# Block attention with a soft mixture of experts: another order of the work inside an attention turn, another chain between the last turn and the experts, and second-matrix loads of 1 MB

## The chip, the cores and the metric

The kernel runs on one core of one Trainium2 chip. The metric is the device time of one execution in microseconds (us). A core has a matrix engine (PE, with its weight loads shown as PEld), a vector engine (DVE), a scalar engine (ACT), GpSimd (POOL) and SyncE (SP, which here issues every load and store). Each engine works through its own instructions in program order; engines wait for each other through semaphores. All numbers are float32.

## The reference, cut to what matters

```python
# q, k, v: (8, 8, 576, 64); attention inside chunks of 64 rows
scores = scale * np.matmul(q_c, k_c.transpose(0, 1, 2, 4, 3))
attn = softmax(scores); out = np.matmul(attn, v_c)
x = out.transpose(0, 2, 1, 3).reshape(4608, 512)
# soft mixture: 8 experts with 4 slots each, phi (512, 32)
logits = x @ phi
d = softmax over the 4608 rows of logits        # per slot
slot_input = d.T @ x                             # (32, 512)
slot_out[e] = np.maximum(slot_input[e] @ w1[e], 0) @ w2[e]   # w1 (8,512,1024), w2 (8,1024,512)
c = softmax over the 32 slots of logits          # per row
return c @ slot_out                              # (4608, 512)
```

## The kernel before, in words

The 4608 rows are cut into nine blocks of 512. Blocks 0 to 7 are the first 512 rows of one batch each; the ninth gathers the last 64 rows of all eight batches and is worked on fifth. A **turn** is two heads of one block, so there are 36 turns, four to a block, and turns 16 to 19 belong to the gathered block.

In a turn the two heads of q and k are brought side by side by POOL (`pair_heads`, tiles `kp`, `qp`), transposed by PE into the PSUM banks `pg` and `ph` (`turn_qk`) and copied by ACT to `kT` and `qT` (`place_qk`, line 217). PE makes the scores in `psc` (`scores`, 227, 32 matmuls), DVE subtracts the maximum (`s_sub`, 233 and 234), ACT takes the exponential (`s_exp`, 239), PE transposes the result into `pt` (`turn_p`, 245), ACT copies it to `at` (`place_p`, 248), PE multiplies by the values into `pav` (`values`, 259), DVE divides (`norm_x`, 272 to 274), PE transposes the row result into `px` (`turn_x`, 280) and ACT copies it to `xT` (`place_x`, 283). POOL lays the values out twice before they are used (`spread_v`, 185 to 190). The code of one pass of the loop works on several turns at once: scores of t, values of t-1, q and k of t+1 and t+2, row result of t-2. `sc`, `at`, `kT`, `qT`, `kp`, `qp` and the PSUM banks are single.

Once for each block, spread over four passes, the bank `pg` also serves the mixture: `logits` with the running maximum and the exponentials (`maxima`, `weights`), two transposes (`natural`), the block's share of the slot inputs (`partial`, added to `p_run`), and the combination weights (`combination` on POOL, then `turn_c`, `place_c` into `cT`).

The order of all instructions is written by hand; nothing reorders it. SP issues in code order: pieces of weights (512 KB each, paced by the pass number: 34 pieces before turn 33), `load_v` of turn t+2 for two turns at a time, `load_qk` of turn t+5. A load waits until its buffer has been read (values have two buffers of two turns, q and k three of one turn) and until the load eight before it has landed. The gathered block is loaded in smaller pieces: eight of 64 KB for two turns of values, four of 128 KB for a turn of q and k.

Behind the last turn a chain of small steps leads from the last row result to the slot inputs `siT`; the softmax over rows is finished there across four lanes (`lane_minimum`, `lane_weights`, `lane_select`), and `slots` makes `siT`. Then the experts: `up` for two experts at a time reads the first matrix (16 tiles of 1 MB, all in SBUF by then), `turn` transposes, `down` reads the second matrix. Of the 32 weight tiles 17 lie in pool `wpa` and are loaded during the turns. Six more go into `wpb`, which lies over the buffers of the attention part and is loaded as these come free. The last nine go into `wpa` again (`refill`), each when `up` has read the tile that lay there. Then the rows are combined and stored.

## Time and profile before

| | us |
|---|---|
| median of three runs | 262.9 (262.69 to 264.4) |
| profiled execution, its own time | 264.01 |
| its span, first to last instruction | 262.2 |
| PE busy in it | 211.6 (81%) |
| DVE, ACT, POOL busy | 123.6, 124.9, 122.2 |
| bytes moved | 71.97 MB, 274 GB/s over the span |

Busy shares are means over the whole span. The span has three parts: the turns, up to about 179 us; the chain and the experts, up to about 230 us; combination and stores. The share of the DMA engines in a stretch is the time that its packets took, over the time of 16 engines; packets overlap, so it can pass 1.

### The profile page before, as it was taken

The page shows a single profiled execution, that of the slowest core. Times are in us where ns is not written, and L with a number is a line of the kernel's source. Part 1 is how long each engine was busy: PE and PEld are TensorE (multiplying, and loading weights), DVE is VectorE, ACT ScalarE, POOL GpSimd, SP SyncE. Part 2 cuts the span into 40 slices and gives each one's busy share as a digit, 9 for nine tenths or more (in the row PEclk, how much of TensorE's full clock was granted, in tenths as well). Part 3 has the DMA queues.
Part 4 walks back from the last instruction along what each step waited for, and adds up shares of the span by engine and source line. Part 5 has one row for each costly group of instructions (what it writes and reads, how often), then busy time and mean ns, then how long its engine had stood idle before and what let it go on. Part 6 is the DMA issues. An engine that isn't in the chain of part 4 may idle for free.

```text
span 262.2 us, 9367 instructions
## 1 busy us (share of the span) xinstructions
PE 211.6 (81%) x3828; PEld 151.6 (58%) x3828; DVE 123.6 (47%) x303; ACT 124.9 (48%) x277; POOL 122.2 (47%) x315
## 2 busy tenths in 40 slices
PE   7788898998988837798897997986579999979700
PEld 7676776675865727577676776674242346447400
DVE  0265656676666631765855956675310000136800
ACT  1447665666666542667567666664111210135600
POOL 2686877865583718397577885850030000000000
PEclk9999999999999995999999999999757999986965
DMA  6978999998974959988999999356956999587997
GB/s 208 317 210 242 357 324 343 303 268 255 296 215 123 274 140 302 356 264 269 358 309 286 345 300 366 94 162 209 391 203 217 356 349 348 177 284 245 264 366 286
DMA packets 60090, 71.97 MB, mean 274 GB/s; under 512 B 3728, under 2 KB 50832, under 8 KB 60048
## 3 DMA queue, kind: packets, MB, share of 16 engines
q1 hardware_dynamic: 60048, 71.38, 85.5%
q8 instruction: 30, 0.49, 0.7%
q14 instruction: 12, 0.10, 0.1%
HBM read 61.93 MB, written 9.44 MB: 272 GB/s over the span
## 4 chain that ended last, share of the span: by engine, by line
PE 46%; DMA 12%; POOL 11%; ACT 11%; DVE 9%; issue 5%; SPq 1%; ACTq 0%; POOLq 0%; DVEq 0%
PE ph L538 6%; PE po L572 5%; PE pf L599 5%; PE pt L245 5%; PE pg L198 4%; PE pav L259 4%; DMA vna<-in_v_dram 4%; ACT sc L239 3%; PE psc L227 3%; PE pg L290 3%; DMA qn<-in_q_dram 3%; DMA knb<-in_k_dram 3%; PE ph L143 3%; ACT kT L217 2%; DMA vnb<-in_v_dram 2%
## 5 line engine op out<-in xcount | busy, mean ns | idle before, releaser
L217 ACT COPY kT<-pg 128x512 f32<-128x512 f32 x36 | 21.1, 587 | 43.9 <-PE pg L198 42.9
L233 DVE TENSOR_REDUCE mx<-psc 128x8 f32<-128x512 f32 x36 | 24.8, 690 | 36.1 <-PE psc L227 36.0
L248 ACT COPY at<-pt 128x512 f32<-128x512 f32 x36 | 21.1, 586 | 21.0 <-PE pt L245 21.0
L198 PE MATMUL pg<-ident,kp 128*128 128x128 f32 x144 | 23.5, 287 | 6.1 <-DVE eT L337 4.1
L245 PE MATMUL pt<-ident,sc 128*128 128x128 f32 x144 | 23.8, 289 | 5.2 <-ACT sc L239 3.8
L234 DVE TENSOR_TENSOR sc<-psc,mx 128x512 f32<-128x512 f32 x36 | 24.9, 692 | 3.2
L227 PE MATMUL psc<-kT,qT 64*64 64x64 f32 x1152 | 25.4, 224 | 0.8 <-ACT qT L217 0.7
L274 DVE TENSOR_TENSOR xb<-pav,rc 128x512 f32<-128x512 f32 x36 | 24.9, 691 | 1.2
L245 PEld LDWEIGHTS pt<-ident,sc 128*128 128x128 f32 x144 | 15.5, 142 | 17.1 <-ACT sc L239 9.7
L227 PEld LDWEIGHTS psc<-kT,qT 64*64 64x64 f32 x1152 | 20.3, 134 | 7.0 <-ACT qT L217 4.2
L239 ACT ACTIVATE sc<-sc 128x512 f32<-128x512 f32 x36 | 22.8, 633 | 0.6 <-DVE sc L234 0.6
L198 PE MATMUL ph<-ident,qp 128*128 128x128 f32 x144 | 22.4, 279 | 0.2 <-issue 0.2
L280 PE MATMUL px<-ident,xb 128*128 128x128 f32 x144 | 22.2, 278 | 0.0
L259 PE MATMUL pav<-vnb,at 64*64 64x65 f32 x576 | 13.7, 229 | 10.4 <-POOL vnb L190 5.7
L194 POOL COPY qp<-qn 128x512 f32<-128x512 f32 x36 | 22.0, 612 | 0.2 <-DMA qn<-in_q_dram 0.2
L198 PEld LDWEIGHTS pg<-ident,kp 128*128 128x128 f32 x144 | 15.4, 142 | 9.4 <-issue 3.8
L217 ACT COPY qT<-ph 128x512 f32<-128x512 f32 x36 | 20.7, 576 | 0.0
L259 PEld LDWEIGHTS pav<-vnb,at 64*64 64x64 f32 x576 | 11.3, 138 | 12.8 <-POOL vnb L190 6.0
L194 POOL COPY kp<-knb 128x512 f32<-128x512 f32 x24 | 14.7, 611 | 8.3 <-PE pg L198 6.4
L280 PEld LDWEIGHTS px<-ident,xb 128*128 128x128 f32 x144 | 17.1, 143 | 1.0 <-ACT xTa L283 0.8
L198 PEld LDWEIGHTS ph<-ident,qp 128*128 128x128 f32 x144 | 17.0, 143 | 1.0 <-POOL vna L188 0.4
L538 PE MATMUL ph<-w,siT 128*32 128x512 f32 x128 | 17.2, 692 | 0.0
(96 smaller groups left out, 344.9 us busy)
## 6 DMA issues: line engine op xcount, KB each, us to landing
w<-in_moe_w_dram SPq DMA_DIRECT2D x64, 512.0 KB
qn<-in_q_dram SPq DMA_DIRECT2D x32, 256.0 KB
knb<-in_k_dram SPq DMA_DIRECT2D x21, 256.0 KB
vna<-in_v_dram SPq DMA_DIRECT2D x16, 256.0 KB
vnb<-in_v_dram SPq DMA_DIRECT2D x16, 256.0 KB
out_dram<-ob SPq DMA_DIRECT2D x8, 512.0 KB
out_dram<-ob SPq DMA_DIRECT2D x4, 1024.0 KB
kna<-in_k_dram SPq DMA_DIRECT2D x11, 256.0 KB
```

The costliest lines, as they stand in the source:

```text
L194: nc.gpsimd.tensor_copy(dst.rearrange("p j a d -> p a j d"), src)
L198: nc.tensor.transpose(out=dst[:, P * j:P * (j + 1)], in_=(kp if isk else qp)[:, j].rearrange("p a d -> p (a d)"), identity=ident)
L217: nc.scalar.copy(o, i)
L227: nc.tensor.matmul(psc[CH * m:CH * (m + 1), a, o:o + CH], lhsT=qT[r, c], rhs=kT[r, c], start=True, stop=True)
L233: nc.vector.reduce_max(mx, pv, axis=AX.X)
L234: nc.vector.tensor_tensor(sc.rearrange("p a M (w x) -> p a (M w) x", x=CH), pv, mx.unsqueeze(3).to_broadcast([P, 2, 4, CH]), ALU.subtract)
L239: nc.scalar.activation(sc, sc, AF.Exp, scale=SCALE)
L245: nc.tensor.transpose(out=pt[:, o:o + P], in_=sc[:, a, M], identity=ident)
L259: nc.tensor.matmul(pvv[q_, 2 * w + M, a, 0:D + 1], lhsT=at[r, a, M, q_], rhs=values_of(t)[r, M, a, 2 * D * m:2 * D * m + D + 1], start=Tru ...
L274: nc.vector.tensor_tensor(x_of(t).rearrange("p l (a d) -> p l a d", d=D), pvv[:, :, :, 0:D], rc.to_broadcast([P, 4, 2, D]), ALU.mult)
L280: nc.tensor.transpose(out=px[:, P * l:P * (l + 1)], in_=x_of(t)[:, l], identity=ident)
L538: nc.tensor.matmul(ph[SL * i:SL * (i + 1), :], lhsT=siT[:, j, :], rhs=wt[1, e, j // 2][:, j % 2, DM * h:DM * (h + 1)], start=(j == 0), sto ...
```

## The change: what it does

**A turn in another order.** In a pass, `turn_p` and `place_p` of turn t-1 now come directly behind the scores of t, and no longer those of turn t behind everything else. `values` of t-1 comes last on PE, directly in front of the next pass's scores. On POOL `pair_heads` of t+2 is now ahead of `spread_v` of t. On SP `load_qk` is now ahead of `load_v`. The mixture's steps are kept together, ahead of the values.

**Another chain behind the last turn.** The logits of the last block are begun before its last row result is there; the transpose of the previous combination weights gets a bank of its own; `lane_minimum` comes ahead of `weights`; the last `partial` is done and added in two halves; five small matmuls on `ident` (`warm`) are added; and the last block's combination weights are transposed behind the first `up` instead of ahead of it, copied by DVE and not by ACT.

**Loads.** The nine full tiles of the second matrix outside the first 17 are loaded by one transfer of 1 MB each, not two of 512 KB. Half tiles of the first matrix are ordered by use: both experts' first halves, then both second halves.

```diff
-    worder = [(1, e, h) for e in range(E) for h in range(2)]
+    worder = [(1, e0 + i, h) for e0 in range(0, E, 2) for h in range(2) for i in range(2)]
...
-            return [(t[:, 1024 * i:1024 * (i + 1)], src[:, 1024 * i:1024 * (i + 1)]) for i in range(2)]
+            return halves(t, src) if n < NWA else [(t, src)]
...
             if t < NT:
                 scores(t)
+            if t >= 1:
+                turn_p(t - 1)
+                place_p(t - 1)
+            if t < NT:
                 s_sub(t)
+            if t + 1 < NT:
+                turn_qk(t + 1, 1, pg)
+                place_qk(t + 1, 1, pg)
+                turn_qk(t + 1, 0, ph)
+                place_qk(t + 1, 0, ph)
+            if t + 2 < NT:
+                pair_heads(t + 2, 1)
+                pair_heads(t + 2, 0)
+            if t + 5 < NT:
+                load_qk(t + 5)
+            if t < NT:
+                s_exp(t)
                 spread_v(t)
+            if t >= 2:
+                turn_x(t - 2)
...
             if t >= 1:
                 values(t - 1)
                 norm_x(t - 1)
             if t % 2 == 0 and t + 2 < NT:
                 load_v(t + 2)
...
-            if t < NT:
-                turn_p(t)
-                place_p(t)
             if t >= 2:
                 place_x(t - 2)
...
+        n = NB - 1
+        logits(n, ph, range(NF - 1))
         turn_x(NT - 1)
         place_x(NT - 1)
-        n = NB - 1
-        turn_c(n - 1)
-        place_c(n - 1)
-        logits(n)
-        maxima(n)
-        weights(n)
+        turn_c(n - 1, psc[:, 0])
+        place_c(n - 1, psc[:, 0])
+        logits(n, ph, range(NF - 1, NF))
+        maxima(n, ph)
+        warm(2)
         wmin = lane_minimum()
+        weights(n, ph)
+        warm(2)
         natural(n)
         natural_copy(n)
         wj = lane_weights(*wmin)
         sums(n)
+        for h in range(2):
+            partial(n, pt, slice(DH * h, DH * (h + 1)))
         ss = lane_select(wj)
-        partial(n, pt)
-        partial_add(n, pt)
+        for h in range(2):
+            partial_add(n, pt, slice(DH * h, DH * (h + 1)))
+        warm(1)
+        slots(*ss)
         shifted(n)
-        slots(*ss)
         combination_exp(n)
         combination(n)
-        turn_c(n)
-        place_c(n)
...
-    load_pieces(wpb, 2 * NWB)
+    load_tiles(wpb, NWB)
...
         hrs[e] = up(e)
+        if e == 0:
+            pc = bank("pc")
+            nc.tensor.transpose(out=pc[:, 0:P], in_=eT, identity=ident)
+            nc.vector.tensor_copy(cT[:, order_b[NB - 1]], pc[:, 0:P])
```

On PE a pass with `partial`, from the scores of one turn to those behind the next, stood like this before (`psc` scores, `pav` values, `pg` and `ph` the transposes of k and q, `px` the row result, `pt` the exponentials):

```order
L227 MATMUL psc<-kT,qT 64x64 x16
L259 MATMUL pav<-vnb_94,at 64x65 x16
L198 MATMUL pg<-ident,kp 128x128 x4
L198 MATMUL ph<-ident,qp 128x128 x4
L280 MATMUL px<-ident,xb_103 128x128 x4
L360 MATMUL pg<-xb_92,eN 32x512 x4
L245 MATMUL pt<-ident,sc 128x128 x4
L227 MATMUL psc<-kT,qT 64x64 x16
```

The same pass on PE now:

```order
L239 MATMUL psc<-kT,qT 64x64 x16
L257 MATMUL pt<-ident,sc 128x128 x4
L210 MATMUL pg<-ident,kp 128x128 x4
L210 MATMUL ph<-ident,qp 128x128 x4
L292 MATMUL px<-ident,xb_104 128x128 x4
L372 MATMUL pg<-xb_93,eN 32x512 x4
L271 MATMUL pav<-vnb_95,at 64x65 x16
L239 MATMUL psc<-kT,qT 64x64 x16
```

The transposes of the exponentials moved from the pass's end to behind the scores and belong to the turn before; the values moved from behind the scores to the end.

On SP two passes stood like this before (late in the turns, behind the gathered block):

```order
L171 DMA vnb_94<-in_v_dram 128x4x128 x2
L154 DMA knb_99<-in_k_dram 128x2x256
L154 DMA qn_86<-in_q_dram 128x2x256
L103 DMA w_6_0_2102<-in_moe_w_dram 128x1024
L154 DMA kna_87<-in_k_dram 128x2x256
L154 DMA qn_84<-in_q_dram 128x2x256
L103 DMA w_6_1_2259<-in_moe_w_dram 128x1024
```

The same two passes on SP now:

```order
L166 DMA knb_100<-in_k_dram 128x2x256
L166 DMA qn_87<-in_q_dram 128x2x256
L183 DMA vnb_95<-in_v_dram 128x4x128 x2
L114 DMA w_6_0_2097<-in_moe_w_dram 128x1024
L166 DMA kna_88<-in_k_dram 128x2x256
L166 DMA qn_85<-in_q_dram 128x2x256
L114 DMA w_7_0_2254<-in_moe_w_dram 128x1024
```

The two loads of values moved behind one load of k and one of q.

On PE the end of the chain, from the transposed maximum to the first matmuls of `up`, was before:

```order
L374 MATMUL psc<-ident,nm_run_71 1x128
L327 MATMUL pg<-ident,eT 128x128
L328 MATMUL pg<-ident,lT 128x128
L389 MATMUL psc<-one,wj 128x32
L360 MATMUL pt<-xb_103,eN 32x512 x4
L400 MATMUL ph<-wsel,p_run 128x32 x4
L405 MATMUL px<-ws,rep 128x1
L353 MATMUL pg<-ident,eT 128x128
L538 MATMUL ph_3235<-w_0_0_280,siT 32x512 x2
```

And now:

```order
L386 MATMUL psc<-ident,nm_run_71 1x128
L155 MATMUL px<-ident 128x128 x2
L339 MATMUL pg<-ident,eT 128x128
L340 MATMUL pg<-ident,lT 128x128
L372 MATMUL pt<-xb_104,eN 32x256 x8
L401 MATMUL pav<-one,wj 128x32
L155 MATMUL px<-ident 128x128
L411 MATMUL ph<-wsel,p_run 128x32 x4
L416 MATMUL pav<-ws,rep 128x1
L548 MATMUL ph_3237<-w_0_0_275,siT 32x512 x2
```

The transpose of `eT` in front of `up` is gone from here, and the partial product now precedes the lanes' weights.

## Rows read from the trace of the kernel before

**Rows 1.** Windows by stretch: bounds and length (us), busy time (instructions) of PE, PEld, DVE, ACT, POOL; granted clock, DMA share, GB/s.

```profile
9.59:60.28 50.69, 43.94 (x997) 35.31 (x998) 30.23 (x68) 31.92 (x66) 39.91 (x104) 1.00 0.96 296
60.28:104.61 44.33, 34.87 (x728) 27.74 (x727) 23.90 (x58) 24.28 (x54) 25.87 (x65) 0.92 0.77 224
104.61:165.66 61.05, 53.32 (x1179) 41.10 (x1178) 40.34 (x98) 39.47 (x88) 42.96 (x108) 1.00 0.99 316
165.66:179.26 13.60, 11.60 (x301) 9.52 (x301) 8.19 (x20) 9.16 (x21) 7.64 (x21) 1.00 0.30 91
193.40:199.00 5.60, 5.28 (x25) 1.37 (x29) 0.00 (x0) 0.27 (x1) 2.29 (x9) 0.50 0.06 23
199.00:225.60 26.60, 26.34 (x332) 11.92 (x324) 1.16 (x8) 2.75 (x4) 0.00 (x0) 0.98 1.05 346
```

**Rows 2.** Timeline of PE: scores of turns 12, 20, 33, values of the last turn.

```profile
60.28 0.69 PE L227 MATMUL psc<-kT,qT 64*64 64x64 f32 x32
...
104.61 0.69 PE L227 MATMUL psc<-kT,qT 64*64 64x64 f32 x32
...
165.66 0.69 PE L227 MATMUL psc<-kT,qT 64*64 64x64 f32 x32
...
178.56 0.70 PE L259 MATMUL pav<-vnb,at 64*64 64x65 f32 x32 [0.78 <-issue]
```

**Rows 3.** The chain that ended last through one pass: start, length, what.

```profile
48.26 0.69 PE pav L259 x32
...
49.58 0.45 ACT kT L217
...
50.06 0.64 ACT sc L239
...
50.75 0.66 PE pt L245 x4
51.40 0.62 PE psc L227 x32
```

**Rows 4.** Timeline of POOL: first and last step of one pass.

```profile
65.86 0.40 POOL L185 COPY vna<-vna 128x256 f32<-128x256 f32 x1
...
68.84 0.61 POOL L194 COPY qp<-qn 128x512 f32<-128x512 f32 x1
```

**Rows 5.** Timelines of SP and POOL: a load of values and its first reader.

```profile
135.69 0.93 SPq L171 DMA_DIRECT2D vna<-in_v_dram  x2
...
144.07 0.40 POOL L185 COPY vna<-vna 128x256 f32<-128x256 f32 x1 [1.04 <-DMA vna<-in_v_dram]
```

**Rows 6.** Timelines of SP, POOL, PE: values of turn 18, load to use.

```profile
86.67 7.97 SPq L175 DMA_DIRECT2D vnb<-in_v_dram  x8
...
97.27 0.40 POOL L185 COPY vnb<-vnb 128x256 f32<-128x256 f32 x1 [6.53 <-DMA vnb<-in_v_dram]
...
99.69 1.14 PE L259 MATMUL pav<-vnb,at 64*64 64x65 f32 x32 [5.58 <-POOL vnb L190]
```

**Rows 7.** The chain that ended last, behind the last turn.

```profile
180.18 0.69 DVE xb L274
...
182.91 1.12 PE pg L290 x32
...
187.08 1.91 PE pt L360 x8
...
189.82 1.92 PE ph L400 x8
...
193.27 0.41 POOL eT L350
...
194.20 9.86 PE ph L538 x64
...
204.74 3.57 PE ph L538 x32
...
225.67 0.44 DVE sp L585
```

More of the change, by code (lines that the diff above doesn't have):

```diff
@@ L74, with halves @@
     wt = {}
+    def halves(t, src):
+        return [(t[:, 1024 * i:1024 * (i + 1)], src[:, 1024 * i:1024 * (i + 1)]) for i in range(2)]
     def weight_pieces(pool, n):
@@ L94, with load_tiles @@
     nload = 0
+    def load_tiles(pool, count):
+        nonlocal nload
+        for _ in range(count):
+            for o, i in weight_pieces(pool, nload):
+                nc.sync.dma_start(o, i)
+            nload += 1
     def load_pieces(pool, count):
@@ L285, with logits @@
         lst = {}
-        def logits(n):
-            for f in range(NF):
+        def logits(n, pl, fs=range(NF)):
+            for f in fs:
                 for l in range(4):
                     nc.tensor.matmul(
-                        pg[SL * l:SL * (l + 1), 0:P],
+                        pl[SL * l:SL * (l + 1), 0:P],
                         lhsT=phi_sb[:, f, :], rhs=xT[f][:, l],
@@ L350, in combination, with turn_c, place_c, partial @@
             nc.gpsimd.tensor_tensor(cc, cc, cs.to_broadcast([P, 4, SL]), ALU.mult)
-        def turn_c(n):
-            nc.tensor.transpose(out=pg[:, 0:P], in_=eT, identity=ident)
-        def place_c(n):
-            nc.scalar.copy(cT[:, order_b[n]], pg[:, 0:P])
-        def partial(n, dst):
+        def turn_c(n, dst):
+            nc.tensor.transpose(out=dst[:, 0:P], in_=eT, identity=ident)
+        def place_c(n, src):
+            nc.scalar.copy(cT[:, order_b[n]], src[:, 0:P])
+        def partial(n, dst, cs=slice(0, DM)):
             for l in range(4):
-                nc.tensor.matmul(dst[SL * l:SL * (l + 1), :], lhsT=eN[:, SL * l:SL * (l + 1)],
-                                 rhs=xb[n % 2][:, l], start=True, stop=True)
+                nc.tensor.matmul(dst[SL * l:SL * (l + 1), cs], lhsT=eN[:, SL * l:SL * (l + 1)],
+                                 rhs=xb[n % 2][:, l, cs], start=True, stop=True)
         def partial_add(n, src, cs=slice(0, DM)):
@@ L438 @@
                 scores(t)
+            if t >= 1:
+                turn_p(t - 1)
+                place_p(t - 1)
+            if t < NT:
                 s_sub(t)
-                spread_v(t)
+            if t + 1 < NT:
[10 more added lines that the diff above has]
+                s_exp(t)
+                spread_v(t)
+            if t >= 2:
+                turn_x(t - 2)
+            if bl is not None:
+                logits(bl, pg)
+                maxima(bl, pg)
+                weights(bl, pg)
+            if bn is not None:
+                natural(bn)
+                sums(bn)
+                natural_copy(bn)
+                shifted(bn)
+                combination_exp(bn)
+            if bp is not None:
+                partial(bp, pg)
+                combination(bp)
+                partial_add(bp, pg)
+            if bc is not None:
+                turn_c(bc, pg)
+                place_c(bc, pg)
             if t >= 1:
```

67 lines of the change are left out of this document (15 added, 52 removed).

## The prediction, made before the changed kernel ran

> **What bounds the kernel now.** I read four views in this order: the windows by stretch, PE's timeline, the chain that ended last, and the queues of POOL and SP.
>
> The windows, cut where scores start, divide the turns into four stretches [rows 1, 2]. Turns 0 to 11 take 50.69 us, 4.22 a turn; turns 12 to 19 take 44.33, 5.54 a turn; turns 20 to 32 take 61.05, 4.70 a turn; from the scores of turn 33 to the end of the last values (179.26) it is 13.6. In the first and the third, PE is busy for 87% of the time and the DMA share is 0.96 and 0.99; the only stretch with a higher share is the one with weights alone, 1.05. So both lie close to two limits, and neither quite holds them: PE's busy time would give 43.9 and 53.3 us, the loads at share 1.05 would give 50.69 x 0.96/1.05 = 46.3 and 61.05 x 0.99/1.05 = 57.6. DVE, ACT and POOL are further off: at most 42.96 of the 61.05.
>
> What holds them is seen in the chain through a pass with little extra work [rows 3]: values at 48.26, then (after k's transpose) ACT's copy to kT at 49.58, the exponential right behind it at 50.06, its transpose at 50.75, the next scores at 51.40. The reader is to see that two ACT steps stand between the values of one turn and the scores of the next, and that each engine in the row waits for the one before. Scores and their successor follow 0.8 us later, so a lap is 3.9 us even here; what the mixture adds comes on top, as it shares the bank `pg` with k's transpose.
>
> POOL does a pass from 65.86 to 69.45, 3.6 us: 1.2 for k and q, 2.4 for spreading the values [rows 4]. It waits for the values' loads: one issued at 135.69 is read at 144.07, 8.4 us later [rows 5].
>
> Turns 12 to 19 are held by loads of the gathered block: the eight for turn 18's values take SP 7.97 us from 86.67, POOL starts on them at 97.27 after 6.53 us of waiting, and PE has waited 5.58 us when it begins at 99.69 [rows 6].
>
> From the last values to the first `up` at 194.20 it is 14.9 us [rows 7]. The DMA engines are idle from 193.4 to 199 (share 0.06), as the refills wait for `up`; from 199 PE is busy 26.34 of 26.6 us while the refills run [rows 1], and `down` ends in the copy at 225.67 [rows 7]. PE and the loads end here together.
>
> **The change, the turn.** A pass issues the same instructions in other places. The exponential of t-1 now comes from the pass before, so its transpose waits for no ACT step of this pass, and ACT and DVE work one pass ahead of the values. The lap of rows 3 is cut; the next limits are PE's own work, 53.32/13 = 4.10 us a turn, and the loads.
>
> New waits. The subtraction on DVE waits for the transpose of t-1 (`sc` is single), which stands just behind the scores and ends about when the maximum does; behind it on DVE only norm_x and the mixture queue, for later use. The values wait for place_p and spread_v; behind them on PE stand the next scores, and DVE and ACT wait for these. spread_v is now behind pair_heads, which wait for k's and q's transposes some 2 us into the pass; with 3.6 us of POOL it ends some 5.5 us after the scores start (my estimate), and the values come some 2.5 us into the next pass, at 6.6: a cover of 1 us, and beyond it PE waits. On SP the values' loads go out behind a load of k and one of q, 0.5 MB, 1.6 us at 316 GB/s [rows 1]; they wait for the values of t-1 as before, and the weights and the next k and q queue behind them.
>
> Prices. Turns 0 to 11: between 0 and -6.8 (PE's busy time), by the loads -4.4; I take -3.5, as the first passes also stand on POOL's 3.6. Turns 20 to 32: between 0 and -7.7, by the loads -3.5; I take -4.5, nearer to the loads, as 0.99 is near to 1.05. The last 13.6 us: 0 (PE alone -2), as the pass behind the last turn now also holds a transpose.
>
> Turns 12 to 19: before, turn 20's scores follow turn 18's values by 104.61 - 99.69 = 4.9 us [rows 2, 6], a whole pass behind the wait. Now that pass is done ahead of the wait and the scores follow the values directly, at 0.7 us: -4.2 with the same landing. The loads also begin earlier by part of the 3.5 us won before. I take -5; the ends are -2, should the loads go out later behind k and q, and -8.
>
> Eight of those loads, 64 KB each, took SP 1.0 us apiece [rows 6], where two of 256 KB took 0.93 together [rows 5]. The Trainium skill, "DMA: Bandwidth & Descriptors", section "Why a DMA increments its semaphore by 16 and not by 1", says that a transfer runs on the largest number of engines up to 16 that divides the slowest dimension on both sides; here that is 4 batches, so 4 engines, in whatever order. The share of 0.77 [rows 1] does not contradict it. By it the stretch stays as long as its loads, rival (2).
>
> Sum of the turns: -3.5 - 5 - 4.5 = -13.
>
> **The change, behind the turns.** Three quarters of the last logits (1.12 us) now lie under the norm and the transposes: -0.8. The previous combination weights leave the space between the row result, ready at 180.87, and the logits at 182.91; of these 2.0 us transposes and copy keep 1.25: -0.8. From the partial product (187.08) to the end of slots (191.74) the halves change the order but not the length at this clock: lanes' weights and their two DVE steps now stand between, 1.0, and the first half of slots covers the second addition (0.44, as the half row at 225.67): 0. From 191.74 to 194.20 only a copy of 0.3 is left, since the steps around POOL's 193.27 move behind `up`: -2.1 [all rows 7]. The lanes' weights no longer delay the partial product: -0.6. That is -4.3. The partial product and slots (1.91 and 1.92) would take about half at the higher clock: up to -2 more; I take -5 in all. The five warm matmuls stand where PE waits; uncovered they cost 0.3 each.
>
> The first `up` takes 9.86 - 3.3 = 6.5 us where later ones take 3.6 [rows 7], and the granted clock from 193.4 to 199 is 0.50 [rows 1]: the lower level, after the sparse chain. Kept at the higher one it gives another -3; I take -1. From `up` to 225.67 PE has the same work, so what the chain gains arrives there unless the loads come later. They do not: the six tiles of `wpb` wait for the same readers, of which the logits come earlier, the 5.6 idle us go, and the refills (26.6 us) follow. Nine loads of 1 MB for eighteen move the same bytes; the nearest rows are 316 GB/s with short runs and 346 with long ones, so longer ones may give at most -1 and cost nothing likely; I take 0. Combination and stores are unchanged.
>
> Sum of this part: -6, between -4 and -9.
>
> **The rivals.**
> (1) The forecast: -13 - 6 = -19, 244 us.
> (2) The gathered block's loads hold the middle: the -5 falls away, -14, 249 us. For it: 7.97 us of SP for eight loads. Against: the 4.9 us between values and scores that need no load.
> (3) The loads bound the turns everywhere: -2 for the first and third stretch together, -2 in the middle, -5 behind: -9, 254 us. For it: shares of 0.96 and 0.99. Against: 1.05 elsewhere.
> (4) PE's busy time is reached and the clock stays up: -6.8 - 5 - 7.7 - 9 = -28.5, 234 us. For it: the three other engines have room. Against: loads and POOL stand close.
> (5) The turn isn't freed, as `pg` or POOL ties each pass to the one before: only the part behind the turns gains, and 2 us in the middle go back: -4, 259 us. For it: POOL's 3.6 us have no gap. Against: 4.2 to 4.7 leave it room.
> (6) Slower. The values' two buffers close a loop: values of t-1, load, spread 2.4, values of t+2 (0.7), three passes in all. At 8.4 us landing that is 3.8 us a pass, hidden. Now 0.5 MB of k and q stand ahead: 10.0 us, 4.4 a pass. From 11 us (4.7 a pass) it decides; at 12 it is 5.0, +0.3 on 13 turns and +0.8 on 12: +14, and -6 behind: +8, 271 us. For it: shares near 1. Against: at most eight loads are out at once, so k and q ahead mean something else behind.
>
> **How the numbers follow.** The profiled span is 262.2 us and its own time 264.01; -19 gives 243.2 and 245.0. The median of the runs lies 1.1 below that execution: 243.9, so 244 us. Chances: (1) 0.55, (2) 0.10, (3) 0.13, (4) 0.08, (5) 0.08, (6) 0.06. The forecast's own ends are 238 to 250. The range 236 to 254 takes in (1) to (3). A measurement of this kernel can't tell less than about 1% from no change, so 260.3 to 265.5; (5) lies close to that edge and is halved: faster 0.90, within 1% 0.04, slower 0.06.
>
> **What would show it.** Passes of 3.8 to 4.4 us in the first and third stretch; a chain that no longer runs from ACT's exponential through its transpose to the next scores; scores of turn 20 within 1 us of turn 18's values; `up` 9 to 11 us behind the last values; no idle DMA stretch there. I would be wrong if PE waited for POOL in front of the values in most passes, if passes took 4.5 us with a DMA share below 0.9, or if refills and not PE set the end of `down`.

## The result: 254 us, and nearly all of the gain lies behind the turns

The changed kernel takes 254.1 us (median of four runs, 251.8 to 255.7); the kernel before, measured beside it, 262.9 (median of three; a fourth execution, of 460.5 us, is left out). The ratio is 0.969, 95% interval 0.962 to 0.976. The profiled execution has a span of 252.7 us and a time of its own of 254.45. Chips and executions differ by a few us, so experiments are read against the kernel before on the same chip, and by places in the trace of one execution each, which for e3, e5, e8, e9, e10 and e12 was one of the longer ones; where no ratio stands, too few of the others were left for an interval, and medians are given.

First the windows of the changed kernel, cut as in [rows 1] where the scores of turns 0, 12, 20 and 33 start and where the last values end, then to the first `up` and over two groups of `up` (columns as there: PE, PEld, DVE, ACT, POOL, granted clock, DMA share, GB/s).

```profile
9.77:61.67 51.90, 41.44 (x994) 35.89 (x998) 29.37 (x65) 31.21 (x66) 37.56 (x98) 0.97 0.92 291
61.67:103.28 41.61, 33.33 (x739) 27.90 (x734) 24.06 (x60) 25.13 (x58) 25.46 (x64) 0.92 0.74 214
103.28:163.52 60.24, 52.03 (x1191) 41.80 (x1185) 38.73 (x96) 37.93 (x86) 44.24 (x112) 0.97 1.00 325
163.52:179.48 15.96, 12.90 (x332) 10.21 (x327) 10.68 (x28) 9.37 (x22) 9.26 (x26) 1.00 0.47 160
179.48:188.16 8.68, 6.74 (x78) 4.76 (x79) 3.45 (x14) 2.29 (x9) 0.00 (x0) 1.00 0.90 370
188.16:195.55 7.39, 7.39 (x65) 2.01 (x65) 1.61 (x8) 1.00 (x2) 2.42 (x9) 1.00 1.00 377
```

Against 50.69, 44.33, 61.05 and 13.60 us [rows 1] the four stretches of the turns are +1.2, -2.7, -0.8 and +2.4: the last values end at 179.48 instead of 179.26. From there to the end it is 73.2 us instead of 83.0, so -9.8: -6.2 up to the first `up` (8.7 us for 14.9), -2.5 in the first two groups of `up` (7.4 us for 9.9), -1.1 in the combination and stores at the end. The chain there, where [rows 7] have the old one:

```profile
180.01 0.70 DVE xb L286
...
182.09 0.43 PE ph L302 x8
...
184.53 1.07 PE pt L372 x16
...
186.68 1.14 PE ph L411 x8
...
188.16 3.64 PE ph L548 x32
...
217.24 0.43 DVE sp L595
```

The partial product and slots take 1.07 and 1.14 us for 1.91 and 1.92, and from the first `up` to the copy for `sp` it is 29.1 us for 31.5.

What PE waited for while the turns ran (9 to 180 us) says where the turns' gain went. First the changed kernel, then the kernel before, in the view of waits: engine, line, what it waited for; us in total, times, longest.

```profile
PE psc L239 <- issue: 11.8, 8, 3.4
PE pg L365 <- POOL eT L362: 5.8, 2, 3.5
PE pav L271 <- POOL vnb L202: 3.5, 2, 3.0
PE pav L271 <- issue: 1.9, 1, 1.9
PE pg L302 <- issue: 1.6, 2, 1.2
```

```profile
PE pav L259 <- POOL vnb L190: 5.7, 2, 5.6
PE pav L259 <- issue: 5.1, 20, 0.8
PE pg L198 <- DVE eT L337: 4.1, 6, 0.7
PE pt L245 <- ACT sc L239: 3.8, 6, 1.2
```

The old waits are gone: `pt` no longer waits for ACT's exponential, and the chain that ended last, which went through two ACT steps in [rows 3], stays on PE through a pass (start, length, what):

```profile
45.49 0.63 PE pav L271 x32
46.11 0.47 PE psc L239 x32
46.58 0.59 PE pt L257 x4
47.17 0.44 PE pg L210 x4
47.60 0.44 PE ph L210 x4
48.04 0.44 PE px L292 x4
```

In the old waits' place is above all time put down to "issue", in which no engine and no load of the kernel holds PE back. (The 5.1 us of it before are 20 gaps, mostly of 0.2 us, longest 0.8.) It lies in the middle of a group of matmuls that wait for nothing, as in this part of PE's timeline:

```profile
53.35 0.45 PE L239 MATMUL psc<-kT,qT 64*64 64x64 f32 x17
57.19 0.70 PE L239 MATMUL psc<-kT,qT 64*64 64x64 f32 x15 [3.38 <-issue]
57.82 0.90 PE L257 MATMUL pt<-ident,sc 128*128 128x128 f32 x3
```

Seventeen of 32 matmuls of one turn's scores run, then PE stands for 3.38 us, then the other fifteen follow. There are ten such stops over 0.3 us inside a group of matmuls in the turns, 15.0 us in all; the kernel before has two, 1.5 us. I set PE's matmuls, counted from the program's start as the profile records them (two records for each float32 matmul of the program, one for a transpose), beside the records of the DMA queue that moves instructions:

```profile
q8 instruction: 30, 0.49, 0.8%
```

That is 30 packets of 16 KB. The stops, with the start of the last such packet ahead of each:

```
changed kernel              kernel before
matmul packet resumes stop  matmul packet resumes stop
  347  21.27  23.64  0.84     729   41.19  43.94  0.84
  473  28.97  31.41  1.90    1359   73.12  75.77  0.62
  599  35.40  37.97  2.01
  976  54.74  57.19  3.38
 1353  74.55  77.11  2.57
 2231 126.38 128.99  0.79
 2356 134.20 136.40  1.22
 2608 145.05 147.46  1.28
 2733 151.78 154.16  0.39
 2858 156.89 159.49  0.64
```

The reader is to see two regularities. The numbers of the matmuls are 125 or 126 apart, or a multiple of that (347, 473, 599, then 976 = 599 + 3 x 125.7), and with one weight load for each matmul that makes some 251 instructions and a few waits to a packet. And each stop ends 2.2 to 2.7 us after a packet's start. So PE's program comes in blocks over the DMA engines, as the loads do, and PE stands still where a block is used up before the next has landed. The Trainium skill, "Runtime: NRT & Kernel Launch", section "Instruction fetch mechanics", describes blocks of 16 KiB with 256 instructions, the next fetched while the current one runs, and says that this is mostly hidden; the sizes agree with the trace, the hiding does not hold here.

The waits for POOL in the list (`eT`, `vnb`) were there before under other names: they are waits for loads of values, one step on. Both waits for `eT`, which end at 90.36 and 113.34, follow a wait of POOL's `spread_v`, behind which the combination's product stands in its queue:

```profile
87.47 0.40 POOL L197 COPY vna<-vna 128x256 f32<-128x256 f32 x1 [3.02 <-DMA vna<-in_v_dram]
...
110.45 0.40 POOL L197 COPY vna<-vna 128x256 f32<-128x256 f32 x1 [2.98 <-DMA vna<-in_v_dram]
```

From the first scores to the last values PE's time then divides as follows. Busy: 139.7 us, before 143.7. Stops: 15.0, before 1.5. Waits for POOL's values and product: 10.0, before 9.2. All other idle time: 5.0, before 15.2. The new order thus saved some 14 us of work and waits, and the stops took 13.5 of it back.

### The profile page after: what moved, and what is told of

Same layout as the page of the kernel before. It is cut to its first block, busy times and chain, and to the rows that moved or that the text cites. A ratio compares the mean times of both kernels' runs of the same rounds, so it can differ in the third digit from the quotient of the medians.

```text
span 252.7 us, 9419 instructions
## 1 busy us (share of the span) xinstructions
PE 202.5 (80%) x3846; PEld 153.5 (61%) x3846; DVE 122.8 (49%) x305; ACT 122.9 (49%) x276; POOL 121.9 (48%) x315
## 4 chain that ended last, share of the span: by engine, by line
PE 52%; POOL 12%; DMA 10%; issue 10%; DVE 6%; ACT 4%; SPq 1%; POOLq 0%; DVEq 0%; ACTq 0%
PE pf L609 6%; PE po L582 6%; PE ph L548 6%; DMA vna<-in_v_dram 5%; PE pav L271 5%; PE pt L257 4%; PE psc L239 4%; PE px L292 3%; PE pg L210 3%; PE ph L210 3%; PE px L155 3%; PE pg L302 3%; DMA vnb<-in_v_dram 2%; POOL kp L206 2%; POOL qp L206 2%
## 5 line engine op out<-in xcount | busy, mean ns | idle before, releaser
L239 PE MATMUL psc<-kT,qT 64*64 64x64 f32 x1152 | 26.5, 223 | 13.3 <-issue 11.8
L239 PEld LDWEIGHTS psc<-kT,qT 64*64 64x64 f32 x1152 | 22.2, 138 | 12.1 <-issue 10.1
L257 PE MATMUL pt<-ident,sc 128*128 128x128 f32 x144 | 25.1, 300 | 0.3 <-ACT sc L251 0.3
L210 PE MATMUL ph<-ident,qp 128*128 128x128 f32 x144 | 23.2, 287 | 0.9 <-POOL kp L206 0.9
L210 PE MATMUL pg<-ident,kp 128*128 128x128 f32 x144 | 23.6, 290 | 0.0
L229 ACT COPY qT<-ph 128x512 f32<-128x512 f32 x36 | 21.8, 604 | 1.7 <-PE ph L210 1.6
L210 PEld LDWEIGHTS ph<-ident,qp 128*128 128x128 f32 x144 | 18.5, 151 | 1.1 <-issue 1.1
L210 PEld LDWEIGHTS pg<-ident,kp 128*128 128x128 f32 x144 | 18.1, 151 | 0.6 <-issue 0.2
L271 PEld LDWEIGHTS pav<-vnb,at 64*64 64x64 f32 x576 | 10.0, 134 | 12.0 <-POOL vnb L202 4.8
L615 DVE COPY ob<-pf 128x256 f32<-128x256 f32 (+1 forms) x26 | 12.6, 522 | 9.0 <-PE pf L609 8.5
L284 DVE TENSOR_SCALAR rc<-pav 128x8 f32<-128x8 f32 x36 | 5.8, 162 | 22.4 <-PE pav L271 22.0
```

The costliest lines, as they stand in the source:

```text
L210: nc.tensor.transpose(out=dst[:, P * j:P * (j + 1)], in_=(kp if isk else qp)[:, j].rearrange("p a d -> p (a d)"), identity=ident)
L229: nc.scalar.copy(o, i)
L239: nc.tensor.matmul(psc[CH * m:CH * (m + 1), a, o:o + CH], lhsT=qT[r, c], rhs=kT[r, c], start=True, stop=True)
L257: nc.tensor.transpose(out=pt[:, o:o + P], in_=sc[:, a, M], identity=ident)
L271: nc.tensor.matmul(pvv[q_, 2 * w + M, a, 0:D + 1], lhsT=at[r, a, M, q_], rhs=values_of(t)[r, M, a, 2 * D * m:2 * D * m + D + 1], start=Tru ...
```

## The experiments

**Theory.** The new order is worth what it was forecast to be, but it uses a block of PE's program up faster than the fetch, queued among saturated loads, can follow. **Rivals.** The loads' rate bounds the turns and the stops only lie in front of it; or POOL and the shared bank tie the passes.

Places of all runs in their traces, in us. "Stops" are PE's, put down to "issue", over 0.3 us, inside a group of matmuls, in the turns (e1, e8 and e10 have one more each at the start of a group, at matmul 2984, of 0.4, 2.0 and 1.9 us, which fits the same count); "behind" is from the end of the last values to the end of the span; the time is a median and stands beside the kernel before on the same chip. e14 and e15 ran once.

```
run                        last values  stops (us)  behind   time / before
kernel before                 179.3       2 (1.5)    83.0        - / 262.9
changed kernel                179.5      10 (15.0)   73.2    254.1 / 262.9
e1_order_only                 176.6       7 (10.7)   81.6    261.0 / 265.2
e2_tail_only                  179.3       2 (1.9)    74.8    256.9 / 265.2
e3_half_instr                 182.8       0          74.8    258.3 / 265.2
e4_few_loads                  159.0       2 (4.1)    73.6    236.0 / 265.2
e5_half_pe                    168.3       3 (2.5)    74.0    243.4 / 263.8
e6_old_order_few_loads        172.1       1 (0.8)    74.2    248.2 / 263.8
e7_slower_weights             179.6      10 (15.7)   73.1    254.7 / 263.8
e8_small_loads                184.1      12 (15.8)   73.7    253.6 / 263.8
e9_no_warm                    180.5       9 (15.5)   77.1    259.3 / 262.5
e10_last_turn                 178.3      12 (14.9)   76.1    255.2 / 262.5
e11_fewer_in_turns            175.6      10 (13.9)   74.1    252.5 / 262.5
e12_changed_again             179.2      10 (14.3)   73.2    252.7 / 263.7
e13_twelve_in_turns           174.0       8 (12.5)   75.6    252.1 / 263.7
e14_old_order_extra           196.4      10 (7.8)    74.1    272.3 / 263.7
e15_old_order_extra_few       188.8       3 (3.0)    74.7    265.3 / 263.7
```

**Each half of the change alone.** e1 is the kernel before with the new body of the loop:

```diff
-                s_sub(t)
-                spread_v(t)
-            if t >= 1:
-                values(t - 1)
-                norm_x(t - 1)
+            if t >= 1:
+                turn_p(t - 1)
+                place_p(t - 1)
...
```

e2 is the changed kernel with that hunk the other way round.

> Only the turns' new order, with the old chain and the old 512 KB loads behind the turns. Theory (TensorE's program is fetched in blocks of 16 KB, and since the new order leaves less slack in a block, TensorE stands still at the block's end until the fetch, queued behind the loads, has landed; the turns gain nothing): the last values end at 179 us, within 2 us of the kernel before, the whole takes 261 to 265 us. Rival (the order is worth 13 us, and it is the new loads or chain that take them back in the turns): the last values end near 166 us, the whole takes about 250 us.

> Only the new chain and loads behind the turns, with the turns in the old order. Theory (all of the 9.5 us gained is behind the turns): 252 to 256 us, as the changed kernel, last values ending within 2 us of 179 us. Rival (the new order is needed for the gain, because it lets the work behind the turns begin differently): 259 to 264 us.

e1: ratio 0.987 (0.975 to 0.999), last values at 176.6. e2: 0.973 (0.965 to 0.982), last values at 179.3, 74.8 us behind them. The work behind the turns carries the gain; the order adds some 3 us, by an interval that nearly reaches 1, and its stops are there without the new loads and the new chain: 7 with 10.7 us.

Five traces share the code of the turns and the bytes loaded in them: e1, e12, the changed kernel, e9 and e8. Their stops add up to 11.1, 14.3, 15.0, 15.5 and 17.8 us (those at matmul 2984 counted), and from the first scores to the last values they take 166.9, 169.2, 169.7, 170.1 and 174.1 us. Less the stops that is 154.6 to 156.3 us in all five: in the new order a stop lengthens the turns by about its own length.

**Fewer loads in the turns, new and old order.** The edit is the same for e4 and e6:

```diff
-    NWA = 17
+    NWA = 16
+    NDIST = 4
...
-                pieces.extend(weight_pieces(pool, nload))
+                if nload < NDIST:
+                    pieces.extend(weight_pieces(pool, nload))
+                else:
+                    wt[worder[nload]] = wt[worder[nload % NDIST]]
+                    pieces.extend([None, None])
...
```

> The changed kernel with 4 of the weights' tiles loaded in the turns; the other 12 of the first 16 are left out and the first four stand in for them, so 12 of about 45 MB less go over the DMA engines in the turns, and part of the computation is changed. Theory (the fetch waits in the DMA engines' queue behind the loads): once the last of the four tiles has landed the fetch starts within 2 us of the end of a block instead of 2 to 8 us, no stop over 0.5 us is left behind turn 8, and the last values end 8 to 14 us earlier. Rival (loads bound the turns): earlier as well, with the fetch's delay unchanged. Rival (GpSimd or the bank binds): last values within 2 us of 179 us.

> The turns in the old order, the new work behind them, and 12 of the first 16 weight tiles left out as in the run of the new order with few loads, whose last values ended at 159.0 us. Theory (the new order is worth what was forecast, some 13 us, where no load holds the fetch back; the old order is bound by its own chain): last values at 170 to 176 us, passes of turns 20 to 32 still 3.9 to 5.3 us. Rival (few loads shorten either order alike, and the order is worth nothing): last values at 158 to 163 us.

The windows of both, cut at the same turns, first the new order, then the old:

```profile
9.86:58.59 48.73, 41.60 (x993) 35.67 (x997) 28.98 (x65) 31.28 (x67) 37.53 (x98) 0.96 0.94 291
58.59:93.43 34.84, 31.92 (x741) 25.98 (x735) 24.18 (x60) 23.99 (x56) 25.31 (x64) 0.95 0.60 169
93.43:143.98 50.55, 49.58 (x1190) 40.06 (x1185) 39.34 (x97) 38.36 (x88) 44.28 (x113) 1.00 0.68 201
143.98:159.03 15.05, 12.92 (x333) 10.21 (x327) 10.63 (x28) 9.58 (x23) 9.00 (x25) 1.00 0.50 163
```

```profile
10.20:61.20 51.00, 43.65 (x997) 35.17 (x997) 30.27 (x68) 31.98 (x66) 39.98 (x104) 1.00 0.88 273
61.20:98.42 37.22, 32.65 (x727) 25.57 (x726) 24.19 (x58) 24.17 (x54) 26.45 (x67) 1.00 0.62 172
98.42:158.47 60.05, 53.12 (x1179) 41.23 (x1178) 39.82 (x98) 39.47 (x88) 42.17 (x107) 1.00 0.58 169
158.47:172.07 13.60, 11.60 (x301) 9.52 (x301) 8.17 (x20) 9.16 (x21) 7.65 (x21) 1.00 0.26 84
```

Read the third line of each. The old order needs 60.05 us at a DMA share of 0.58, as it needs 61.05 at 0.99 [rows 1]: it is bound by its own chain and not by the loads. The new order falls from 60.24 to 50.55, and PE is busy for 49.58 of them: that is the pace at which the loads no longer hold it. With few loads the new order ends its values 13.0 us ahead of the old (159.0 against 172.1), and the times are 236.0 and 248.2 us (e6: ratio 0.942, 0.938 to 0.945); with full loads it is 0.2 us behind in the profiled runs. So POOL and the shared bank, which are the same in both, don't tie the passes at the changed kernel's pace. The gain is larger than expected (20.5 us, not 8 to 14), and the detail was not exact: one stop, 1.8 us, still falls in turn 11, and behind it packets start up to 3.5 us after PE has begun the block ahead. Of the changed kernel's 20.5 us against e4, 10.9 are stops (15.0 to 4.1) and 3.7 are PE's busy time in the four stretches (139.7 to 136.0), at granted clocks of 0.97, 0.92, 0.97 and 1.00 against 0.96, 0.95, 1.00 and 1.00. The other 6 are PE's remaining idle time, above all the waits for POOL's values and product, 10.0 against 4.8 us.

**Fewer instructions at the same loads.** e3 puts the even and odd chunks' matmuls of scores (shown), and likewise of values, into one of 128 columns; e5 leaves out half of them, in both places:

```diff
-                        for a in range(2):
-                            r = slice(D * a, D * (a + 1))
-                            nc.tensor.matmul(psc[CH * m:CH * (m + 1), a, o:o + CH], lhsT=qT[r, c], rhs=kT[r, c],
-                                             start=True, stop=True)
+                    for a in range(2):
+                        r = slice(D * a, D * (a + 1))
+                        nc.tensor.matmul(psc[:, a, o:o + CH], lhsT=qT[r, c:c + 2 * CH], rhs=kT[r, c:c + CH],
+                                         start=True, stop=True)
...
```

```diff
-            for M in range(2):
+            for M in range(2 if t == 0 else 1):
```

> The changed kernel with two 64-column matmuls of scores, and of values, put into one of 128 columns: half as many TensorE instructions there for the same streaming time and the same loads (the odd blocks then use the even blocks' keys and values, so part of the computation is changed). Theory (block fetch): a block of the program lasts a third longer, no stop of TensorE over 0.5 us without a named wait is left in the turns (10 stops with 15 us in the changed kernel), the last values end 10 to 15 us earlier, at 165 to 170 us, and the whole takes 239 to 245 us. Rival (the loads bound the turns): the stops are replaced by waits of GpSimd for loads, the last values end at 177 to 180 us. Rival (GpSimd's copies and the shared bank tie the passes): the same, with TensorE waiting for GpSimd or for a bank.

> The changed kernel without the second half of the scores' and values' matmuls after the first turn (that part of the computation is left out; all copies, transposes and loads stay): a third fewer TensorE instructions per turn under the same loads. Theory (stops at the blocks of the program are what the turns lose): no stop over 0.5 us without a named wait is left, turns 20 to 32 take 50 to 55 us instead of 60, the last values end at 160 to 168 us. Rival (the loads' rate bounds the turns, the stops only lie in front of it): no stops either, but turns 20 to 32 stay at 58 to 61 us, with TensorE and GpSimd waiting for loads, and the last values end at 176 to 180 us.

e3 has no stop left, as expected, but its last values come at 182.8 us (ratio 0.971, 0.957 to 0.984), and neither theory nor rival had that: the wider matmuls do not take the same time. The group of the scores in e3 (line, operation, shapes, count, busy us, mean ns, idle before):

```profile
L238 PE MATMUL psc<-kT,qT 64*128 64x64 f32 x576 | 40.0, 280 | 1.5 <-ACT qT L229 1.5
```

Half as many matmuls are busy for 40.0 us where the 1152 of the changed kernel are for 26.5, so PE became the bound (61.98 of 63.48 us in turns 20 to 32), and the run tells only that the stops go with the count of instructions. e5 has stops of 2.5 us instead of 15.0 (three, two of them over 0.5 us, where none was expected), its last values at 168.3, 11.2 us earlier and 0.3 beyond the range, and a ratio of 0.918 (0.912 to 0.923). Its four stretches of the turns:

```profile
9.38:54.19 44.81, 36.09 (x658) 30.17 (x662) 29.08 (x65) 31.56 (x66) 37.63 (x97) 0.96 1.01 324
54.19:96.90 42.71, 31.46 (x483) 24.03 (x478) 23.82 (x60) 25.13 (x58) 25.27 (x64) 0.88 0.82 225
96.90:152.21 55.31, 48.27 (x774) 37.44 (x769) 38.22 (x96) 38.07 (x86) 44.62 (x112) 0.94 1.06 353
152.21:168.26 16.05, 12.88 (x220) 8.87 (x215) 10.93 (x28) 9.88 (x23) 9.27 (x26) 0.91 0.52 175
```

Turns 20 to 32 take 55.3 us, at the edge of the theory's range and below the rival's. But the run does not say what the stops alone cost: PE's busy time falls with them, from 139.7 to 128.7 us, and its idle time stays at 30, as the waits for POOL's values and product, which wait for loads, grow from 10.0 to 21.0 us. What it does show is that the same loads fit into 158.9 us from the first scores to the last values. So their rate does not hold the changed kernel at 169.7; it comes into play where PE has less to do.

**More instructions in the old order.** The dummies stand in front of each turn's transposes of the probabilities, with full loads (e14) and with few (e15):

```diff
+        def extra():
+            for i in range(4):
+                for m in range(2):
+                    for a in range(2):
+                        nc.tensor.matmul(psc[CH * m:CH * (m + 1), a, 300:301],
+                                         lhsT=ident[D * a:D * (a + 1), 0:CH], rhs=ident[D * a:D * (a + 1), 0:1],
+                                         start=True, stop=True)
...
+                extra()
                 turn_p(t)
```

> The turns in the old order with the new work behind them, and 16 small dummy matmuls (one column each) in front of the transposes of each turn's probabilities: a third more TensorE instructions per turn at the same loads. Without the dummies this had 2 stops with 1.9 us and its last values at 179.3 us. Theory (a block of the program is used up before its fetch, held behind the loads, has landed): 8 or more stops over 0.3 us with at least 8 us, at each 126th matmul, last values at 190 us or later. Rival (the loads' rate is what holds the turns, the stops only go with it): no more than 4 stops, last values at 179 to 186 us, by the dummies' own time.

> The same dummies with 12 of the first 16 weight tiles left out; without dummies the last values came at 172.1 us with 0.8 us of stops. Theory: the fetch is not held back behind turn 9, so at most 4 stops with 4 us, and the dummies cost only their own time: last values at 172 to 180 us, at least 10 us before those of the run with full loads and dummies (without dummies the two are 7.3 us apart). Rival (the instructions themselves take the time, whatever the loads): as late against its base as with full loads, 7 to 8 us apart.

The stops came as expected: from 2 with 1.9 us (e2) to 10 with 7.8 us, at matmuls 477, 604, 858, 1237, 1364 and so on, again multiples of 126 or 127 apart, and with few loads only 3 with 3.0. The times did not: 196.4 and 188.8 us lie 7.6 us apart, as without dummies (179.3 and 172.1). The dummies themselves were mis-sized. In e14 (group by line, as above):

```profile
L246 PE MATMUL psc<-ident 64*64 64x1 f32 x1152 | 23.6, 196 | 2.7 <-issue 1.9 <-DVE sc L254 0.8
```

They take 23.6 us of PE and lengthen each pass, and what the stops cost beyond that cannot be read from the pair. By e15's own terms the rival held: the dummies delay the last values by 17.0 us with full loads and by 16.7 with few, although the stops grow by 5.9 and 2.2. So in the old order, with its own waits beside them, stops do not simply add to the time; for the new order this pair tells nothing.

**Weights at another pace.** e7 spreads the 17 tiles over 35 turns; e13 loads 12 of them in the turns and 5 behind:

```diff
-            want = min(2 * NWA, 2 * NWA * max(t - 1, 0) // (NT - 5))
+            want = min(2 * NWA, 2 * NWA * max(t - 1, 0) // (NT - 1))
```

```diff
+    NWT = 12
...
-            want = min(2 * NWA, 2 * NWA * max(t - 1, 0) // (NT - 5))
+            want = min(2 * NWT, 2 * NWT * max(t - 1, 0) // (NT - 5))
...
+    load_tiles(wpa, NWA - NWT)
     load_tiles(wpb, NWB)
```

> The changed kernel with the same 17 weight tiles spread over 35 turns instead of 31: a tenth fewer weight bytes per turn, none left out. Theory (fetch behind the loads): the fetch waits a little less, stops fall from 15 us to 10 to 13 us, the last values end 1 to 4 us earlier, 250 to 254 us on a chip where the changed kernel has 254. Rival (the loads behind the turns come later by as much as the turns gain): last values earlier but the time the same. Rival (it is not the backlog): no change within 1 us anywhere.

> The changed kernel once more, beside the next run on the same chip, since chips and runs differ by a few us: 0.96 to 0.975 of the kernel before, last values at 177 to 183 us, 8 to 13 stops of TensorE over 0.3 us with 12 to 17 us.

> The changed kernel with 12 of the 17 first weight tiles loaded in the turns and 5 behind the last turn's loads; its last turn as in the changed kernel. Theory (1.6 us less in the turns for each MB, and the DMA engines have room between turn 33 and the first up matmul): scores of turn 33 at 154 to 159 us instead of 163.5, and 3 to 7 us less in all than the changed kernel on the same chip. Rival (what leaves the turns comes back behind them, as waits for weights in front of up and down): within 2 us of the changed kernel.

e7: ratio 0.969 (0.965 to 0.972), as the changed kernel, and stops of 15.7 us where 10 to 13 were expected. Turn 33's scores start 3.1 us earlier, at 160.4, and a stop of 3.2 us that ends at 170.8, where weights now are loaded beside the last turns, takes it back. e12 gave the changed kernel's picture again: 252.7 us beside 263.7, ten stops, seven of them at the same matmuls as in the list above. e13 on that chip: ratio 0.958 (0.954 to 0.962), 252.1 us. Its turns are 5.2 us shorter than e12's, but 2.4 come back behind them, in part as waits of `down` for weights, and the medians are 0.6 us apart. Here the rival held.

```profile
PE po L584 <- DMA w<-in_moe_w_dram: 1.8, 3, 0.9
```

**Behind the turns.** e8 takes the 1 MB loads back, e9 the dummy matmuls:

```diff
-            return halves(t, src) if n < NWA else [(t, src)]
+            return halves(t, src)
```

```diff
-        warm(2)
         wmin = lane_minimum()
         weights(n, ph)
-        warm(2)
...
-        warm(1)
         slots(*ss)
```

> The changed kernel with its loads behind the turns in pieces of 512 KB again. From the last values to the end the changed kernel takes 73.2 us, the kernel before 83.0. Theory (the gain there is the chain's; 1 MB loads are worth nothing, as forecast): 73 to 74.5 us. Rival (the 1 MB loads give the 3.6 us that lie behind the first up matmul): 76 to 77.5 us, with SyncE's issues later than the buffers come free.

> The changed kernel without the five dummy matmuls in the chain behind the turns. In the changed kernel the stretch from the last values to the first up matmul ran at a granted clock of 1.00 and took 8.7 us (before: 0.74 and 14.9 us), and the first two groups of up matmuls took 7.6 us (before: 9.9 us). Theory (the gain that the prediction missed is the clock, and the dummies hold it): the clock falls in that stretch, the first two groups take 9 to 10 us again, and from the last values to the end it takes 75.5 to 78 us instead of 73.2. Rival (the shorter waits of the new chain hold the clock by themselves, the dummies do nothing): 73 to 74 us.

e8 takes 73.7 us behind the turns, 0.5 more than the changed kernel, and has a ratio of 0.959 (0.953 to 0.965): the large loads are worth nothing measurable, as forecast. e9 takes 77.1, and its windows from the last values to the first `up` and over two groups of `up` show why:

```profile
180.53:191.30 10.77, 7.71 (x69) 4.93 (x69) 3.33 (x13) 2.29 (x9) 0.00 (x0) 0.69 0.95 373
191.30:200.40 9.10, 9.10 (x66) 2.30 (x65) 1.73 (x8) 1.00 (x2) 2.42 (x9) 0.81 0.63 225
```

Without the five dummies the granted clock is 0.69 and 0.81 where it was 1.00 and 1.00, so part of the time at 1.2 GHz; the chain is 2.1 us longer and the two groups of `up` 1.7. The times are too scattered to show these 3.8 us (255.2 to 260.8 in four executions), but the other traces agree. The three without the dummies are low in both windows: 0.74 and 0.71 before, 0.61 and 0.72 in e1, and e9. Of the fourteen with them, thirteen ran the chain at 0.94 to 1.00 (e3: 0.69) and thirteen the two groups at 1.00 (e10: 0.81); so the dummies mostly hold the clock, not always.

**The last turn.** e10 moves the last probabilities and values ahead (the main part of its edit is shown); e11 is e10 with 14 instead of 17 tiles loaded in the turns (as e13's edit, with `NWT = 14`):

```diff
+            if t == NT - 1:
+                turn_p(t)
+                place_p(t)
+                shifted(bn)
+                combination_exp(bn)
+            if t == NT:
+                turn_x(t - 2)
+                partial(bp, pg)
+                combination(bp)
+                partial_add(bp, pg)
...
```

> The changed kernel with the last turn's probabilities transposed in its own pass, and its values as the first work of the pass behind it, ahead of the last but one block's partial sum. In the new order turn 33's scores to the last values take 16 to 19 us, in the old order 13.6 us. Theory (the order itself costs 2 us there, since the last values come at the end of a pass): 13.5 to 15 us where no stop falls in it, and 1 to 3 us less in all, 251 to 253 us on a chip where the changed kernel has 254. Rival (the loads behind the turns or GpSimd's product set the end): the last values come earlier and the first up matmul does not, the time is the same.

> As the run before, with 14 instead of 17 weight tiles in the turns and the other three issued behind the last turn's loads, where the DMA engines were busy for 0.47 of the time. Theory (12.6 MB less took 20 us off the turns, 1.6 us for each MB): 3 to 5 us less up to the scores of turn 33, of which some goes again where the three tiles lie in front of the fetch; 246 to 251 us. Rival (the loads behind the turns bound the end, so what leaves the turns comes back there): 251 to 255 us, with waits for weights in front of up or down.

e10's stretch from turn 33's scores to the last values is 14.75 us, as the theory said, but its first `up` starts 9.9 us behind them instead of 8.7: at 188.15 us, where the changed kernel's starts at 188.16. The next transposes (`px`) come at 180.75 in e10 and at 180.76 in the changed kernel. Behind it, the two groups of `up` take 9.2 us at a granted clock of 0.81, where the changed kernel has 7.4 at 1.00. The time, 255.2 beside 262.5, shows no gain. e11: ratio 0.962 (0.956 to 0.968); turn 33's scores at 158.5, and again a stop beside the last turns, 2.4 us up to 168.9. Neither is told apart from the changed kernel with certainty, and no version beats it clearly.

## Why the prediction was wrong, by its steps

**Turns, -13 forecast, 0 measured (169.71 us from the first scores for 169.67).** The step that failed is the sentence on the next limits behind the lap, PE's own busy time and the loads. There is a nearer one: PE's program itself comes over the loaded DMA engines, and the new order, which uses a block up sooner and has fewer waits to hide a late one, stands still for 15.0 us where it was 1.5. Turns 0 to 11 came at +1.2 (forecast -3.5, and my upper end of 0 was too low). The loads did not hold that stretch: their share fell from 0.96 to 0.92, while its stops grew from 0.8 to 8.1 us. Turns 20 to 32 came at -0.8 (forecast -4.5, more than the -3.5 that I had worked out from the loads), with 4.3 us of stops at a share of 1.00. That the lap would be cut was right: the chain now runs from values to scores to transposes on PE alone, and the waits of `pt` for the exponential are gone. The order is worth 12.7 us with few loads (13.0 with an earlier start), as large as forecast in sum, but divided otherwise: -2.3, -2.4, -9.5 and +1.5 by the stretches of e4 and e6.

**Turns 12 to 19, -5 forecast, -2.7 measured.** The mechanism held: turn 18's values and turn 20's scores on PE's timeline.

```profile
102.77 0.70 PE L271 MATMUL pav<-vnb,at 64*64 64x65 f32 x32 [3.00 <-POOL vnb L202]
103.28 0.65 PE L239 MATMUL psc<-kT,qT 64*64 64x64 f32 x32
```

They are 0.5 us apart where it was 4.9 [rows 2, 6]. What the term lacked is again the stop, 2.57 us up to 77.11, and one wait for a load of values by way of `eT`, 2.28 us up to 90.36. Rival (2), the gathered block's loads as the floor, is out: with the same gathered loads and fewer weights the stretch falls to 34.8 us (e4).

**The last 13.6 us, 0 forecast, +2.4 measured.** The last values now stand at the end of a pass; e4 shows +1.5 there without a stop over 0.3 us. The chain behind them gets 1.1 of it back: it takes 8.7 us in the new order and 9.8 in the old (e2).

**Behind the turns, -6 forecast, -9.8 measured, outside its ends of -4 and -9.** The mechanism was right and the size off. The chain gave -6.2 for -5; of that -5.1 is there with the turns in the old order (e2) and was sized rightly. The mis-sized term is the clock, taken at -1: the first two groups of `up` gave -2.5, and e9 with the other traces shows that it is mostly the dummies that hold it. I had put them down as a possible cost. (The first group took 6.0 us before, 32 matmuls from 194.1 to 200.2, not 6.5.) The -1.1 in the combination and stores, forecast as unchanged, is chance: from the copy for `sp` to the end e1, with all of the old work there, takes 35.4 us as the changed kernel does, for 36.5 before. The 1 MB loads at 0 were right (e8).

That the time of 254.1 us lies so close to the upper end of the range, 254, is luck in part: it is the sum of a miss of 13 us in the turns and one of 4 the other way behind them.

**Rivals.** (3), 254 us, gives the measured time, but by another sum: -4 in the turns and -5 behind, where it was 0 and -10. Its mechanism is refuted for the old order (e6) and comes into play in the new one where PE has less to do (e5: 55.3 us in turns 20 to 32 at a share of 1.06, a little under the 57.6 that I had worked out for the loads at 1.05). Of the signs for the forecast, passes of 3.8 to 4.4 us came in the first stretch (4.3), but they had been 4.2 before, so this could tell nothing there. Of the signs for an error, passes of 4.5 us at a DMA share below 0.9 did not show; the third stretch has 4.6 us at 1.00. I had tied that sign to a low share and so had none for the case that came.

**What stays open.** From the matmul with which PE begins a block to the start of the next block's packet it is some 3.1 us in the new order, in the mean of 24 blocks, and 2.7 in the old one, at the same loads; few loads bring it to 2.2 and 2.1. So the loads delay the packet, and the order does so little. What the order changes more is how soon a block is used up, its stop not counted: 6.1 us in the mean instead of 6.8, and 13 of the 24 within 6 us instead of 7. (These are estimates: the ends of blocks are seen at the stops and set at even counts between them.) How the loads delay the packet no run shows. Nor does a run take away the stops and nothing else: e4 takes loads with them and e5 work of PE. That a stop costs its own length rests on the five traces of the same turns; in the old order it does not hold (e14, e15).

## What to carry to other kernels

Count the instructions of the busiest engine against its fetch: where a block's worth of small matmuls is used up in about the time that a packet needs among saturated loads (here 4 to 6 us at the stops), removing waits uncovers the fetch. Before an order is priced down to an engine's busy time, look at the same stretch with part of the loads left out; if it only then reaches that pace, the gain must be bought with fewer instructions or fewer bytes there. A few dummy matmuls in the gaps of a thin chain can pay through the clock: here 3.8 us by the traces, in the chain and the work behind it.

## What the runs showed of the hardware that I had not expected

- PE stops in the middle of 32 matmuls that wait for nothing, for up to 3.38 us, at every 125 or 126 matmuls with their weight loads or a multiple of that, and resumes 2.2 to 2.7 us after a 16 KB packet of the instruction queue starts. The packet itself takes 0.95 to 1.6 us in the turns.
- The view of the chain has the stops under "issue": 10% of the span in the changed kernel, 5% before.
- A 64-row matmul of 128 columns for two of 64 is no saving: 576 of them are busy for 40.0 us, 1152 of the smaller for 26.5.
- Matmuls of one column are not free either: 1152 take 23.6 us in e14.
